# GpSimd's product of q held behind VectorE's keys, and a second scan tile, in a gated linear attention with a feed-forward layer

## The chip, the cores and the metric

One core of one Trainium2 chip runs the whole kernel. The metric is the device time of one execution in microseconds (us). TensorE is called PE, VectorE DVE, ScalarE ACT, GpSimd POOL, and SyncE, which issues most DMAs, SP, as in the profile.

## The reference

```python
for t in range(S):
    state = alpha[:, :, t, :, None] * state + np.einsum('bhd,bhe->bhde', k[:, :, t], v[:, :, t])
    y[:, :, t] = np.einsum('bhd,bhde->bhe', q[:, :, t], state)
...
h = x @ w_in
g = 0.5 * h * (1.0 + erf(h * inv_sqrt2))
return (g @ w_out).astype(np.float32)
```

There are 4 batches, 8 heads, 768 steps and head dimension 48; alpha lies between 0.8 and 1. The attention's output, as 3072 tokens by 384, goes through a feed-forward layer with 2048 hidden units, all in float32.

## The kernel before

**Attention in units.** Tokens are cut into 12 groups of 256, three to a batch. A group has two units of four heads each; unit n is u = n % 2 of group g = n // 2, so there are 24. In names of `pp`, `rp`, `pe`, `s` and `ss`, such as `pp_7_1`, the first figure is the group and the second is u (here unit 15); in those of `hp`, `ghi` and `glo` they are group and hidden slice. A last figure only tells buffers apart. For each unit:

- DVE makes running products of alpha forward (`pp`, two scans, L283), takes the last of them (L287, L289), makes running products backward (`rp`, two scans, L304), and multiplies k by `rp` in place. This last product is called the keys (L309).
- q is multiplied by `pp` into a tile `qk` (L299): on DVE in units 0 to 5, on POOL from unit 6 on, the late units. There are three `qk` tiles in turn, so the product of unit n needs the tile that unit n - 3 has read for the last time.
- PE makes scores from `qk` and the keys (L325), DVE masks them (`ss`, L340), PE multiplies them by v (L399) and makes the sums for the states (L426), DVE adds the states up (L452, L454), and PE multiplies q by the states (L487, the outer part). ACT and DVE turn the result into the high and low parts of x (L541, L545).

**Late units on PE come in visits.** The visit of unit n runs, in this order, L399 of unit n, L426 of unit n + 1, L325 of unit n + 2, a short POOL memset called `done` that waits for PE (L842), and L487 of unit n, which waits for that memset.

**Feed-forward in steps.** A step `3_4` is hidden slice 4 of group 3. gemm1 (L572, 18 matmuls) fills `hp`; ACT takes the gelu twice, to `ghi` (L593) and in place (L594); DVE makes `glo`, their difference (L599); gemm2 (L622, 12 matmuls) multiplies `ghi` by the weights' high and low parts and then, in its last four matmuls, `glo`.

**The order is written out by a planner.** `plan_unit` makes an `Op` for every piece of work with an engine, a cost, dependencies and a rank. A loop places them on PE, DVE, ACT, SP and POOL by costs from a table (`COST`, for example 1.35 for POOL's product, 0.65 for keys), and the instructions are issued in the order planned. So one dependency more moves work on other engines too. On the chip only semaphores hold an instruction: within an engine the order is fixed, across engines each waits for the data that it uses and for the buffers that it writes. `pp` and `rp` have one buffer each. In the plan the first forward scan of a unit waits for the product of the unit before, since that product reads `pp`:

```python
pp = work.tile([P, 2, G], F32, tag="pp", bufs=1, name=f"pp_{g}_{u}")
...
d["first"] = op("DVE", "scan", start, [d["load"], p.get("q"), p.get("back")], rank=r)
...
before = pp_.get("outer") if n < NU * NSB + 2 else unit[n - 3].get("outer")
d["q"] = op(e, cost, lambda: fns["q"](), [d["scan"], d["rest"], before], rank=r)
```

Here `p` is the unit before, `pp_` the one before that, and `before` the outer part of unit n - 3. The keys are not among the product's dependencies.

Of the kernel before, what the change touches and what calls it, by code (L numbers as in the profile page):

```python
# [8 lines left out]
F32 = mybir.dt.float32  # L9
# [6 lines left out]
ALU = mybir.AluOpType  # L16
AX = mybir.AxisListType
PSUM = bass.MemoryType.PSUM
# [12 lines left out]
LANES = 8  # L31
RATE, ALONE, LATENCY, SMALL, BEGIN = 350e3, 290e3, 2.1, 50e3, 2.2
MARGIN = 1.5
HOME = {0: 0, 1: 1, 2: 2, 4: 1, 5: 0, 6: 2, 8: 1, 9: 0, 10: 2, "s": 1}
X_GAP, Z_GAP, HI_GAP, LO_GAP, LATE_GAP = (128, 0, 192), 0, (64, 0), (0, 64), 0
COST = dict(
    scan=0.65, back=0.72, keys=0.65, q=1.35, qv=0.62, scores=1.0, kn=0.5, mask=0.62, inside=1.05, chain=1.15, outer=0.85, carry=0.26, last=0.34, last_p=0.15, sums=0.55, scaled=0.45,
# [7 lines left out]
def gla_then_gelu_ffn(ctx: ExitStack, tc: tile.TileContext, q, k, v, alpha, akq, w_in, w_out, out):  # L45
    nc = tc.nc
    B, H, D, S = q.shape
    NF, P, NK, _ = w_in.shape
# [3 lines left out]
    G = 2 * C  # L52
    CS = C // 2
# [3 lines left out]
    NU = NPAIR // 2  # L57
# [4 lines left out]
    NSB = GPB  # L62
# [78 lines left out]
    for half in range(2):  # L141
        r = slice(half * CS, (half + 1) * CS)
        nc.gpsimd.affine_select(
            out=mask[r],
# [16 lines left out]
    late = []  # L161
# [107 lines left out]

    cur = {}  # L270

    def ahead(g, u):
        at, kt, qt = (data[g % NB][:, u, n] for n in range(3))
        pp = work.tile([P, 2, G], F32, tag="pp", bufs=1, name=f"pp_{g}_{u}")
        rp = work.tile([P, 2, G], F32, tag="rp", bufs=1, name=f"rp_{g}_{u}")
        pe = work.tile([P, 2], F32, tag="pe", bufs=6, name=f"pe_{g}_{u}")
        cur[g, u] = dict(pe=pe, kt=kt)

        def by_chunk(x):
            return x.rearrange("p i (j t) -> p i j t", t=CS)  # L280

        def forward(i):
            nc.vector.tensor_tensor_scan(pp[:, i], at[:, i], top, MID, ALU.mult, ALU.min)  # L283

        def last():
            eng = nc.vector if g >= NSB else nc.gpsimd
            eng.tensor_scalar(out=pe, in0=pp[:, :, G - 1], scalar1=BOTTOM, scalar2=None, op0=ALU.max)  # L287
            if g >= NSB:
                nc.vector.reciprocal(rp[:, :, G - 1], pe)  # L289

        def queries():
            n = NU * g + u
            if len(qk) == NU and n >= NU * NSB + 2:
                to_late()
                qk.append(late[0].tile([P, 2, NCH, KW], F32, tag="qk2", name="qk2"))
                put_eye(qk[-1])
            qs = cur[g, u]["qs"] = qk[u if g < NSB else n % (NU + 1)]
            eng = nc.vector if g < NSB else nc.gpsimd
            eng.tensor_tensor(out=qs[:, :, :, :CS], in0=by_chunk(qt), in1=by_chunk(pp), op=ALU.mult)  # L299

        def backward(i):
            if g < NSB and i == 0:
                nc.vector.reciprocal(rp[:, :, G - 1], pe)
            nc.vector.tensor_tensor_scan(  # L304
                rp[:, i, G - 2 :: -1], at[:, i, G - 1 : 0 : -1], top[:, 1:], rp[:, i, G - 1 :], ALU.mult, ALU.min
            )

        def keys():
            nc.vector.tensor_tensor(out=kt, in0=kt, in1=rp, op=ALU.mult)  # L309

        return forward, queries, backward, last, keys

# [456 lines left out]
    def op(*args, **kw):  # L769
        ops.append(Op(*args, **kw))  # L770
        return ops[-1]
# [4 lines left out]
    def plan_unit(n):  # L776
# [21 lines left out]
        else:  # L798
            d["v"] = p["v"]
        pool = g < NSB  # L800
        d["first"] = op("DVE", "scan", start, [d["load"], p.get("q"), p.get("back")], rank=r)
        d["scan"] = op("DVE", "scan", lambda: fns["f"](1), [d["first"]], rank=r)
        d["last"] = op("POOL" if pool else "DVE", "last_p" if pool else "last", lambda: fns["l"](), [d["scan"]], rank=r)
        e, cost = ("DVE", "qv") if pool else ("POOL", "q")
# [7 lines left out]
        d["back"] = op("DVE", "keys", lambda: fns["k"](), [d["b1"], d["rest"]], rank=r)  # L812
        if pool:
            d["b0"].cost += 0.17
        ready = [d["back"], d["q"], p.get("mask"), p.get("kn")]
        if pool or n == NU * NSB:
            d["scores"] = op("PE", "scores", lambda: scores(g, u), ready, rank=r)
# [345 lines left out]
```

## Time and profile before

| what | value |
|---|---|
| median of 3 runs | 503.26 us (502.67 to 503.4) |
| the profiled execution | 503.02 us |
| its span | 501.0 us |
| PE busy | 487.1 us, 97% |
| DVE busy | 301.7 us, 60% |
| POOL busy | 34.8 us, 7% |
| mean granted PE clock | 0.995 of full speed |

Times in the trace count from the start of the span. A row of a timeline gives start, duration, engine, line, operation, what is written and read, and how many instructions; in brackets stands the engine's idle time before, and what ended it. Matmuls overlap, so the duration of a row is not the step from one matmul to the next.

### The profile page before, as it was taken

What the parts mean: (1) busy time and instruction counts of PE and PEld (TensorE: products, weight loads), DVE (VectorE), ACT (ScalarE), POOL (GpSimd) and SP (SyncE); (2) the same over time, 40 slices, a digit from 0 to 9 for tenths busy, and PEclk for the clock granted to TensorE, in tenths of its full rate; (3) what the DMA queues carried; (4) which work ended last, traced back from release to release, by engine and by line L of the source; (5) the groups of instructions that cost most, each with busy time, mean ns of one, the idle gap of its engine ahead of it and who ended that gap; (6) DMA issues with size and microseconds to landing.
All of it is one profiled execution on the core that took longest, in us unless ns stands there. A gap on an engine that the chain in (4) does not pass through costs nothing.

```text
span 501.0 us, 13833 instructions
## 1 busy us (share of the span) xinstructions
PE 487.1 (97%) x5970; PEld 474.9 (95%) x5970; DVE 301.7 (60%) x580; ACT 217.9 (43%) x467; POOL 34.8 (7%) x69
## 2 busy tenths in 40 slices
PE   7898999999999999999999999999999999999996
PEld 7777899999998999998999999999999999999996
DVE  6999999999789999899266264251232211211211
ACT  2776856645445555555352352351332222222221
POOL 4100011000111121211010011000000000000000
PEclk9998999999999999999999999999999999999999
DMA  8967363531024453344031020010010000000001
GB/s 299 391 189 236 123 234 128 188 128 65 0 89 147 139 170 120 103 163 143 1 86 60 2 82 2 0 49 2 1 46 4 0 33 1 33 0 1 33 0 37
DMA packets 17153, 44.20 MB, mean 88 GB/s; under 512 B 2240, under 2 KB 8512, under 8 KB 17088
## 3 DMA queue, kind: packets, MB, share of 16 engines
q1 hardware_dynamic: 16656, 42.87, 25.3%
q8 instruction: 49, 0.80, 0.7%
q10 hardware_dynamic: 432, 0.39, 0.3%
q14 instruction: 16, 0.13, 0.1%
HBM read 36.18 MB, written 4.72 MB: 82 GB/s over the span
## 4 chain that ended last, share of the span: by engine, by line
PE 85%; DVE 9%; issue 2%; ACT 1%; DMA 1%; SPq 0%; DVEq 0%
PE acc L622 38%; PE hp L572 38%; PE s L325 3%; PE ybank L399 2%; PE ybank L487 2%; DVE rp L304 2%; DVE pp L283 2%; PE ybank L426 2%; DMA akq<-in_akq_dram 1%; DVE qk L299 1%; DVE ss L340 1%; DVE x L545 1%; DVE glo L599 1%; DVE akq L309 0%; DVE states L454 0%
## 5 line engine op out<-in xcount | busy, mean ns | idle before, releaser
L572 PE MATMUL hp<-x,wih 128*128 128x256 f32 x1152 | 202.5, 278 | 0.0
L572 PEld LDWEIGHTS hp<-x,wih 128*128 128x128 f32 x1152 | 179.2, 189 | 0.6
L572 PE MATMUL hp<-x,wil 128*128 128x256 f32 x576 | 159.8, 278 | 0.0
L599 DVE TENSOR_TENSOR glo<-hp,ghi 128x512 fp32r<-128x512 f32 x92 | 63.1, 686 | 160.4 <-ACT hp L594 160.3
L593 ACT ACTIVATE ghi<-hp 128x512 fp32r<-128x512 f32 x96 | 57.4, 598 | 197.7 <-PE hp L572 197.4
L622 PE MATMUL acc<-woh,ghi 128*128 128x384 f32 x384 | 130.9, 341 | 0.0
L622 PE MATMUL acc<-wol,ghi 128*128 128x384 f32 x384 | 128.9, 336 | 0.0
L572 PEld LDWEIGHTS hp<-x,wil 128*128 128x128 f32 x576 | 108.9, 189 | 0.0
L622 PE MATMUL acc<-woh,glo 128*128 128x384 f32 x384 | 82.5, 335 | 2.0 <-DVE glo L599 2.0
L622 PEld LDWEIGHTS acc<-woh,ghi 128*128 128x128 f32 x384 | 72.1, 188 | 1.7
L622 PEld LDWEIGHTS acc<-wol,ghi 128*128 128x128 f32 x384 | 72.1, 188 | 0.0
L622 PEld LDWEIGHTS acc<-woh,glo 128*128 128x128 f32 x384 | 67.8, 188 | 2.8 <-DVE glo L599 2.7
L594 ACT ACTIVATE hp<-hp 128x512 f32<-128x512 f32 x96 | 56.9, 593 | 0.0
L304 DVE TENSOR_TENSOR_SCAN rp<-akq,rp,top 128x255 f32<-128x255 f32 x48 | 35.8, 774 | 0.8
L283 DVE TENSOR_TENSOR_SCAN pp<-akq,top 128x256 f32<-128x256 f32 x48 | 31.0, 679 | 3.9 <-POOL qk L299 2.0
L299 POOL TENSOR_TENSOR qk<-akq,pp 128x512 f32<-128x512 f32 x18 | 24.8, 1380 | 45.8 <-DVE pp L283 15.5
L325 PE MATMUL s<-qk,akq 48*64 48x112 f32 x768 | 23.9, 260 | 2.3 <-DVE akq L309 1.1
L541 ACT CAST x<-ybank 64x256 fp32r<-64x256 f32 (+4 forms) x60 | 20.0, 333 | 9.4 <-PE ybank L487 5.0
L334 ACT COPY kn<-s 128x384 f32<-128x384 f32 x24 | 11.5, 480 | 28.9 <-DVE ss L340 16.3
L454 DVE TENSOR_TENSOR states<-ybank,states 128x96 f32<-128x96 f32 x66 | 16.8, 255 | 10.1 <-ACT x L541 7.8
L309 DVE TENSOR_TENSOR akq<-akq,rp 128x512 f32<-128x512 f32 x24 | 22.2, 926 | 0.7
L325 PEld LDWEIGHTS s<-qk,akq 48*64 48x64 f32 x768 | 19.3, 133 | 3.2 <-issue 1.5
(79 smaller groups left out, 390.3 us busy)
## 6 DMA issues: line engine op xcount, KB each, us to landing
akq<-in_akq_dram SPq DMA_DIRECT2D x22, 768.0 KB, 5.2
st<-in_moe_w_in_dram SPq DMA_DIRECT2D x8, 768.0 KB, 4.4
st<-in_moe_w_out_dram SPq DMA_DIRECT2D x8, 768.0 KB, 4.9
vn<-in_v_dram SPq DMA_DIRECT2D x12, 384.0 KB, 4.9
out_dram<-part SPq DMA_DIRECT2D x11, 384.0 KB, 3.0
x<-z SPq DMA_DIRECT2D x63, 32.0 KB, 1.9
akq<-in_akq_dram SPq DMA_DIRECT2D x2, 512.0 KB, 5.2
akq<-in_akq_dram SPq DMA_DIRECT2D x2, 256.0 KB, 4.5
```

Of the source, the lines that this page charges most:

```text
L283: nc.vector.tensor_tensor_scan(pp[:, i], at[:, i], top, MID, ALU.mult, ALU.min)
L299: eng.tensor_tensor(out=qs[:, :, :, :CS], in0=by_chunk(qt), in1=by_chunk(pp), op=ALU.mult)
L304: nc.vector.tensor_tensor_scan(rp[:, i, G - 2 :: -1], at[:, i, G - 1 : 0 : -1], top[:, 1:], rp[:, i, G - 1 :], ALU.mult, ALU.min)
L309: nc.vector.tensor_tensor(out=kt, in0=kt, in1=rp, op=ALU.mult)
L325: nc.tensor.matmul(d["s"][o, h, e : e + KW], lhsT=d["kt"][r, i, t], rhs=d["qs"][r, i, j], start=True, stop=True)
L454: d["chain"] = nc.vector.tensor_tensor(out=st[j + 1], in0=new, in1=st[j], op=ALU.add)
L541: nc.scalar.copy(hi, y)
L572: nc.tensor.matmul(hp[:, j, :], lhsT=a[:, j, i * P : (i + 1) * P], rhs=x[:, i, :], start=(j == 0 and i == 0 and n == 0), stop=(i == NK - 1 ...
L593: nc.scalar.activation(ghi, hp, AF.Gelu)
L594: nc.scalar.activation(hp, hp, AF.Gelu)
L599: nc.vector.tensor_tensor(out=glo, in0=hp, in1=ghi.bitcast(F32), op=ALU.subtract)
L622: nc.tensor.matmul(acc[t], lhsT=a[:, j, t * C : (t + 1) * C], rhs=w[:, j, :], start=(first and j == 0 and k == 0 and w is wo_hi[f]), stop= ...
```

## The change

Three things change, all for late units. The instruction of POOL's product gets a dependency on the keys of its own unit, and so does its `Op` in the plan. The odd units from 11 on take their `pp` from a pool on the side that the weights' conversion has left (`late`), so that `pp` of an odd and of an even unit are two tiles. In the plan the first forward scan then waits for the product of two units before, where either this unit or the one before has the second tile, which is so from unit 11 on.

```diff
--- before.py
+++ after.py
@@ -31,6 +31,7 @@
 LANES = 8
 RATE, ALONE, LATENCY, SMALL, BEGIN = 350e3, 290e3, 2.1, 50e3, 2.2
 MARGIN = 1.5
+OTHER_FROM = 11
 HOME = {0: 0, 1: 1, 2: 2, 4: 1, 5: 0, 6: 2, 8: 1, 9: 0, 10: 2, "s": 1}
 X_GAP, Z_GAP, HI_GAP, LO_GAP, LATE_GAP = (128, 0, 192), 0, (64, 0), (0, 64), 0
 COST = dict(
@@ -269,9 +270,13 @@
 
     cur = {}
 
+    def other_products(n):
+        return n >= OTHER_FROM and n % 2 == 1
+
     def ahead(g, u):
         at, kt, qt = (data[g % NB][:, u, n] for n in range(3))
-        pp = work.tile([P, 2, G], F32, tag="pp", bufs=1, name=f"pp_{g}_{u}")
+        room = late[0] if other_products(NU * g + u) else work
+        pp = room.tile([P, 2, G], F32, tag="pp", bufs=1, name=f"pp_{g}_{u}")
         rp = work.tile([P, 2, G], F32, tag="rp", bufs=1, name=f"rp_{g}_{u}")
         pe = work.tile([P, 2], F32, tag="pe", bufs=6, name=f"pe_{g}_{u}")
         cur[g, u] = dict(pe=pe, kt=kt)
@@ -296,7 +301,14 @@
                 put_eye(qk[-1])
             qs = cur[g, u]["qs"] = qk[u if g < NSB else n % (NU + 1)]
             eng = nc.vector if g < NSB else nc.gpsimd
-            eng.tensor_tensor(out=qs[:, :, :, :CS], in0=by_chunk(qt), in1=by_chunk(pp), op=ALU.mult)
+            ins = eng.tensor_tensor(out=qs[:, :, :, :CS], in0=by_chunk(qt), in1=by_chunk(pp), op=ALU.mult)
+            if g >= NSB:
+                tc.add_manual_dep(
+                    ins.ins,
+                    cur[g, u]["keys"].ins.name,
+                    mybir.DependencyInfo(mybir.DependencyClass.Sync, mybir.DependencyReason.DATA),
+                    reason="beside instructions that read PSUM",
+                )
 
         def backward(i):
             if g < NSB and i == 0:
@@ -306,7 +318,7 @@
             )
 
         def keys():
-            nc.vector.tensor_tensor(out=kt, in0=kt, in1=rp, op=ALU.mult)
+            cur[g, u]["keys"] = nc.vector.tensor_tensor(out=kt, in0=kt, in1=rp, op=ALU.mult)
 
         return forward, queries, backward, last, keys
 
@@ -798,7 +810,7 @@
         else:
             d["v"] = p["v"]
         pool = g < NSB
-        d["first"] = op("DVE", "scan", start, [d["load"], p.get("q"), p.get("back")], rank=r)
+        d["first"] = op("DVE", "scan", start, [d["load"], (p if not other_products(n) and not other_products(n - 1) else pp_).get("q"), p.get("back")], rank=r)
         d["scan"] = op("DVE", "scan", lambda: fns["f"](1), [d["first"]], rank=r)
         d["last"] = op("POOL" if pool else "DVE", "last_p" if pool else "last", lambda: fns["l"](), [d["scan"]], rank=r)
         e, cost = ("DVE", "qv") if pool else ("POOL", "q")
@@ -812,6 +824,8 @@
         d["back"] = op("DVE", "keys", lambda: fns["k"](), [d["b1"], d["rest"]], rank=r)
         if pool:
             d["b0"].cost += 0.17
+        else:
+            d["q"].deps.append(d["back"])
         ready = [d["back"], d["q"], p.get("mask"), p.get("kn")]
         if pool or n == NU * NSB:
             d["scores"] = op("PE", "scores", lambda: scores(g, u), ready, rank=r)
```

The sequence of instructions on POOL stays as it was. On DVE, ACT, PE and SP the planner gives other places to some. Line numbers of the changed program are higher: the forward scan is L288, `pe` L292, its reciprocal L294, POOL's product L304, the backward scan L316, keys L321, scores L337, L399 is L411, L426 is L438, states L464 and L466, the outer part L499, gemm1 L584, `glo` L611 and gemm2 L634.

The listing shows the scans as SCALAR_TENSOR_TENSOR. First, DVE between the visits of units 10 and 13, from the forward scans of unit 15 on. Before:

```order
L283 SCALAR_TENSOR_TENSOR pp_7_1_2804<-akq1_119,top_113 128x256 x2
L287 TENSOR_SCALAR pe_7_1_2806<-pp_7_1_2804 128x2
L289 RECIPROCAL rp_7_1_2805<-pe_7_1_2806 128x2
L304 SCALAR_TENSOR_TENSOR rp_7_1_2805<-akq1_119,rp_7_1_2805,top_113 128x255 x2
L309 TENSOR_TENSOR akq1_119<-akq1_119,rp_7_1_2805 128x512
L599 TENSOR_TENSOR glo_3_5_2899<-hp_3_5_2808,ghi_3_5_2894 128x512
L452 COPY states1_132<-ybank_137 128x96
L454 TENSOR_TENSOR states1_132<-ybank_137,states1_132 128x96 x3
```

With the change, from the keys of unit 14 on:

```order
L321 TENSOR_TENSOR akq1_119<-akq1_119,rp_7_0_2616 128x512
L288 SCALAR_TENSOR_TENSOR pp_7_1_2689<-akq1_119,top_113 128x256 x2
L292 TENSOR_SCALAR pe_7_1_2691<-pp_7_1_2689 128x2
L294 RECIPROCAL rp_7_1_2690<-pe_7_1_2691 128x2
L316 SCALAR_TENSOR_TENSOR rp_7_1_2690<-akq1_119,rp_7_1_2690,top_113 128x255
L611 TENSOR_TENSOR glo_3_4_2766<-hp_3_4_2668,ghi_3_4_2760 128x512
L316 SCALAR_TENSOR_TENSOR rp_7_1_2690<-akq1_119,rp_7_1_2690,top_113 128x255
L464 COPY states0_131<-ybank_137 128x96
```

Before, the forward scans of unit 15 stood behind the reads of a visit, and their backward scans, keys and then `glo` of step 3_5 followed each other. Now they stand directly behind the keys of unit 14, `glo` of step 3_4 stands between the two backward scans, and the keys of unit 15 come later.

Second, PE at the visit of unit 10, from the matmul ahead of it on. Before:

```order
L572 MATMUL hp_3_2_2496<-x3_1973,wil2_148 128x256
L399 MATMUL ybank_137<-ss_5_0_2303,vn1_118 64x64 x16
L426 MATMUL ybank_137<-vn1_118,kn_127 64x48 x12
L325 MATMUL s_6_0_2551<-qk0_120,akq0_117 64x112 x16
L487 MATMUL ybank_137<-qk1_121,states0_131 48x64 x16
L572 MATMUL hp_3_3_2593<-x3_1973,wih3_141 128x256 x2
```

With the change:

```order
L584 MATMUL hp_3_3_2523<-x3_1973,wil3_149 128x256
L411 MATMUL ybank_137<-ss_5_0_2302,vn1_118 64x64 x16
L438 MATMUL ybank_137<-vn1_118,kn_127 64x48 x12
L337 MATMUL s_6_0_2578<-qk0_120,akq0_117 64x112 x16
L499 MATMUL ybank_137<-qk1_121,states0_131 48x64 x16
L634 MATMUL acc0_3_0_2437<-woh2_156,ghi_3_2_2542 128x384
```

Before, the visit stood behind gemm1 of step 3_2 and ahead of gemm1 of step 3_3; now it stands behind both, and gemm2 of step 3_2 follows it at once.

Third, PE at the visit of unit 11. Before:

```order
L399 MATMUL ybank_137<-ss_5_1_2463,vn1_118 64x64 x16
L426 MATMUL ybank_137<-vn0_116,kn_127 64x48 x16
L325 MATMUL s_6_1_2707<-qk1_121,akq0_117 64x112 x16
L487 MATMUL ybank_137<-qk2_1849,states1_132 48x64 x16
L622 MATMUL acc0_3_0_2437<-woh3_157,ghi_3_3_2640 128x384
```

With the change:

```order
L411 MATMUL ybank_137<-ss_5_1_2462,vn1_118 64x64 x16
L438 MATMUL ybank_137<-vn0_116,kn_127 64x48 x16
L337 MATMUL s_6_1_2726<-qk1_121,akq0_117 64x112 x16
L499 MATMUL ybank_137<-qk2_1849,states1_132 48x64 x16
L634 MATMUL acc0_3_0_2437<-woh4_158,ghi_3_4_2760 128x384
```

The visit was followed by gemm2 of step 3_3 and is now followed by gemm2 of step 3_4, since the visits of units 10 and 11 stand one step later among the steps.

## Rows read from the trace of the kernel before

**Rows 1.** The page's head: span, and busy time of PE, the weight load and VectorE.
```profile
span 501.0 us, 13833 instructions
...
PE 487.1 (97%) x5970; PEld 474.9 (95%) x5970; DVE 301.7 (60%) x580; ACT 217.9 (43%) x467; POOL 34.8 (7%) x69
```

**Rows 2.** Busy time in stretches of 20 us; columns as in the first row.
```profile
core 0: us, PE busy (x) PEld busy (x) DVE busy (x) ACT busy (x) POOL busy (x), PEclk, DMA share, GB/s
...
220.00:240.00 20.00, 18.96 (x262) 18.36 (x252) 17.55 (x36) 8.85 (x22) 2.79 (x3) 1.00 0.34 109
...
380.00:400.00 20.00, 20.00 (x147) 20.00 (x146) 3.94 (x7) 5.44 (x10) 0.00 (x0) 1.00 0.00 1
```

**Rows 3.** Waits of PE: who for whom, us in total, times, longest.
```profile
PE acc L622 <- DVE glo L599: 2.0, 2, 1.0
```

**Rows 4.** POOL's product of q by its line: duration in ns, min/median/max.
```profile
L299 POOL TENSOR_TENSOR qk<-akq,pp x18: 1290/1306/1737, 63.2 to 300.5; 128x512 f32<-128x512 f32 x18
```

**Rows 5.** VectorE's backward scans by their line: duration in ns, min/median/max.
```profile
L304 DVE TENSOR_TENSOR_SCAN rp<-akq,rp,top x48: 721/745/1832, 6.5 to 300.1; 128x255 f32<-128x255 f32 x48
```

**Rows 6.** VectorE's keys by their line, columns as above.
```profile
L309 DVE TENSOR_TENSOR akq<-akq,rp x24: 684/692/1691, 7.9 to 300.9; 128x512 f32<-128x512 f32 x24
```

**Rows 7.** Timeline of VectorE from 149 to 232 us.
```profile
start us, us, engine line op out<-in xcount [idle before <-releaser]
149.61 0.67 DVE L599 TENSOR_TENSOR glo<-hp,ghi 128x512 fp32r<-128x512 f32 x1
150.19 1.23 DVE L309 TENSOR_TENSOR akq<-akq,rp 128x512 f32<-128x512 f32 x1
...
158.34 1.83 DVE L304 TENSOR_TENSOR_SCAN rp<-akq,rp,top 128x255 f32<-128x255 f32 x1
160.09 0.66 DVE L599 TENSOR_TENSOR glo<-hp,ghi 128x512 fp32r<-128x512 f32 x1
...
164.73 0.69 DVE L309 TENSOR_TENSOR akq<-akq,rp 128x512 f32<-128x512 f32 x1
165.33 1.27 DVE L283 TENSOR_TENSOR_SCAN pp<-akq,top 128x256 f32<-128x256 f32 x2
...
229.56 1.61 DVE L309 TENSOR_TENSOR akq<-akq,rp 128x512 f32<-128x512 f32 x1
231.09 0.68 DVE L599 TENSOR_TENSOR glo<-hp,ghi 128x512 fp32r<-128x512 f32 x1
```

**Rows 8.** Timeline of PE at two waits and at one visit (start, us).
```profile
160.81 0.44 PE L622 MATMUL acc<-woh,glo 128*128 128x384 f32 x1 [0.99 <-DVE glo L599]
...
165.78 0.69 PE L399 MATMUL ybank<-ss,vn 64*64 64x64 f32 x32
...
166.75 0.95 PE L325 MATMUL s<-qk,akq 48*64 48x112 f32 x30
...
168.07 0.44 PE L622 MATMUL acc<-woh,ghi 128*128 128x384 f32 x1
...
231.82 0.97 PE L622 MATMUL acc<-woh,glo 128*128 128x384 f32 x4 [1.04 <-DVE glo L599]
```

**Rows 9.** Timeline of POOL in the same stretch; in brackets its idle time before.
```profile
149.57 1.30 POOL L299 TENSOR_TENSOR qk<-akq,pp 128x512 f32<-128x512 f32 x1 [1.06 <-PE ybank L487]
...
158.32 1.30 POOL L299 TENSOR_TENSOR qk<-akq,pp 128x512 f32<-128x512 f32 x1 [1.09 <-PE ybank L487]
...
185.72 1.74 POOL L299 TENSOR_TENSOR qk<-akq,pp 128x512 f32<-128x512 f32 x1 [1.09 <-PE ybank L487]
...
211.86 1.72 POOL L299 TENSOR_TENSOR qk<-akq,pp 128x512 f32<-128x512 f32 x1 [1.09 <-DMA x<-z]
...
229.30 1.32 POOL L299 TENSOR_TENSOR qk<-akq,pp 128x512 f32<-128x512 f32 x1 [1.12 <-PE ybank L487]
```

**Rows 10.** Waits of POOL: us in total, times, longest.
```profile
POOL qk L299 <- PE ybank L487: 12.3, 11, 1.4
```

## Prediction

> **What bounds the kernel now.** I read the head of the page first: PE is busy for 487.1 of 501.0 us [rows 1]. So a change on POOL and DVE can give only what PE waits for them, or take what it makes PE wait. Second, the busy time by stretches: from 220 to 240 us DVE is busy for 17.55 of 20 us and PE has lost 1.04, while from 380 to 400 DVE has 3.94 us of work and PE loses nothing [rows 2]. The change can act only while late units are made, and there DVE has little to spare. Third, the waits of PE: for `glo` it waited twice, 2.0 us in all [rows 3]. Fourth, the timelines, for what made `glo` late. One backward scan took 1.83 us where the median is 745 ns; it started at 158.34, beside a product that ran from 158.32 to 159.62, and the `glo` behind it started at 160.09 [rows 5, 7, 9]. PE sat idle for 0.99 us and went on at 160.81 [rows 8]. The second wait is alike: keys took 1.61 us from 229.56, beside a product from 229.30 to 230.62, `glo` began at 231.09, and PE waited 1.04 us [rows 7 to 9]. So an instruction of DVE with both inputs in SBUF (a scan, the keys) is held while POOL's product runs. The price of a meeting is 1832 - 745 = 1.09 us for a scan [rows 5] and up to 1691 - 692 = 1.00 us for keys [rows 6]. `glo`, which reads one input from PSUM, took 0.67 us at 149.61 beside the product of 149.57 [rows 7, 9]: it isn't held. When DVE is first, POOL waits: products of 1.74 and 1.72 us against a median of 1.306, 0.42 more [rows 4, 9].
>
> **What is removed.** The product no longer runs beside backward scans and keys of its own unit, so the two meetings that made PE wait are gone: -2.0 us [rows 3]. That is all there is to gain. Other keys were held too (1.23 us at 150.19 [rows 7]), but PE didn't wait for `glo` after them.
>
> **What is added: the product is later.** It starts when its unit's keys end, and PE's scores wait for it. At unit 11 the keys ended at 164.73 + 0.69 = 165.42 and the bulk of the visit's scores started at 166.75 [rows 7, 8], 1.33 us later. A product of 1.306 us [rows 4] just fits; one that first lets a scan by takes 1.74 [rows 9], 0.41 too long. DVE and PE both come there about 1 us earlier with the change, so their distance stays. The next forward scan starts at 165.33, before the keys end [rows 7], so DVE is first: I take 0.4, between 0 and 0.4. Behind the waiting product on POOL stands the visit's `done`, and behind that PE's outer part; scores wait in the same visit already, so this adds nothing. In the unit after it the second forward scan meets the rest of the product and loses about the 1.0 us that its backward scan no longer loses: no change, between -1 and +1 in DVE's time, with gemm work as cover.
>
> **What is moved.** From unit 11 on two tiles of `pp` let DVE run one unit ahead: forward scans stand directly behind the keys of the unit before (the first of the places shown). The keys of a unit are then done before the visit that gives back its `qk` tile, and the product waits for that visit as it does today, when PE's outer part ended its wait 11 times, some 1.1 us before its start [rows 9, 10]. It then runs beside the scans or keys of the **next** unit, which nothing in the change keeps apart from it. So meetings are as many as before, about one to a visit; what counts is whether the held instruction stands ahead of the `glo` that gemm2 directly behind the visit needs. In both waits of today it did. I find three such places in the new order, where the product of unit n is let go by the visit of unit n - 3. After the visit of unit 11 the product of unit 14 meets the first backward scan of unit 15, and `glo` of step 3_4 is next, for the gemm2 shown behind that visit. After the visit of unit 13 the product of unit 16 meets a backward scan of unit 17; the unit's keys stand between it and the `glo` that is needed. After the visit of unit 15 the product of unit 18 meets the keys of unit 19, with `glo` directly behind. The first and third I price as the two measured waits, 1.0 us each [rows 8]. The second costs 1.0 and the keys' 0.60 us (164.73 to 165.33 [rows 7]): 1.6. Sum 3.6. Each can also be nothing, as when the scan starts first and POOL waits, or as much as a hold and keys, 1.7 us; so 0 to 5.1.
>
> On the size of a hold the row and the notes differ a little. The Trainium skill, SBUF — State Buffer, section Who interferes with whom, says that the second to issue fully blocks until the first has finished; a scan that starts with the product would then take 1.306 + 0.745 = 2.05 us, and by that three waits would be 0.7 us dearer in all. The row of 158.34 shows 1.83, and I go by it.
>
> Without effect: the second tile itself; the moves of visits and conversions between 64 and 130 us, where PE waits for nothing and the same work stays on each engine; swapped loads and stores on SP, since the operands that they bring are used many steps later. Work on PE is the same, with as many visits, and after the last visit gemm work alone is left to the end, as in the stretch from 380 us [rows 2].
>
> **Sum.** -2.0 + 0.4 + 3.6 = +2.0 us. On the profiled execution's 503.02 us that is 505.0. The median of the runs is 0.24 higher, 503.26, so the forecast for it is **505.3 us**. A measurement of this kernel tells about 0.2%, 1.0 us, from no change.
>
> **Rivals.**
> - *It does what its words say, and PE's waits go.* If keys really come last, the product runs beside `glo`, states and masks, and DVE gets its holds back. For it: `glo` isn't held, and the two waits are both of this kind. Against it: the new order puts forward scans, not reads of PSUM, behind the keys of units 11, 12, 14, 15 and 18. The decisive point is whether the keys of units 14 to 18 end after the outer part that frees the tile. Result: 503.26 - 2.0 = 501.3 us; with one of the three waits, 502.3. The Trainium skill, same page and section, says that an instruction with at most one SBUF input doesn't contend with GpSimd; by that alone this rival would come true, and the trace agrees with it for `glo`.
> - *As many waits as before.* Two of the three places make PE wait 1.0 us, the scores nothing: -2.0 + 2.0, 503.3 us, between 502.3 and 504.2. For it: not all held keys cost PE a wait today, and 0.1 us decides whether DVE or POOL comes first. Against it: the second place has two instructions ahead of `glo`.
> - *Everything waits.* Three dear places and the scores: -2.0 + 0.4 + 5.1 = +3.5, 506.8 us. For it: DVE has some 10% to spare in these visits, so it doesn't make up a hold by the next visit.
>
> **How the numbers follow.** I give 0.62 to slower by over 1.0 us (my forecast, about 504.3 to 506.4 by itself, and the last rival, 0.10 of it), 0.24 to as many waits, 0.14 to the first rival. The range reaches from 502.0, which leaves out most of the first rival, to 507.0, just over the last.
>
> **What would show it.** Right: in the trace after, PE's waits for `glo` number three or so and sum to over 3 us, each behind a scan or keys of over 1 us beside a product; POOL's product is still let go by PE's outer part in units 14 to 18; scores of unit 11 wait for POOL. Wrong: products start with the end of keys everywhere, scans and keys stay near 745 and 692 ns, and PE's waits for `glo` are gone. If holds stay and PE doesn't wait, my choice of places is wrong; if PE waits elsewhere, for the masks or for x, a move that I costed at nothing is.

## The result, and the profile after

The change made the kernel slower: 508.02 us median of 6 runs (506.6 to 509.2) against 503.06 us (502.43 to 503.62) for the kernel before in the same measurement, a ratio of 1.0096 with a 95% interval of 1.0075 to 1.0117. That is 5.0 us; 2.0 were forecast, and the range ended at 507.0. The profiled execution took 506.6 us, so it is the quickest of the six, and a part of what the median lost need not be in it. The two executions of the change with a mean granted PE clock of 0.999, the profiled one among them, took 506.6 and 506.7 us, and the four with 0.993 to 0.997 took 507.8 to 509.2.

The head of the page, against [rows 1]:

```profile
span 504.7 us, 13831 instructions
PE 487.6 (97%) x5970; PEld 474.4 (94%) x5970; DVE 301.5 (60%) x580; ACT 217.2 (43%) x467; POOL 35.7 (7%) x69
```

PE's work is about the same (487.1 before), so what was lost are PE's waits. From 60 to 260 us they are (line waited for, us in total, times, longest), against [rows 3]:

```profile
PE acc L634 <- DVE glo L611: 3.8, 2, 2.4
PE hp L584 <- DMA x<-z: 1.4, 1, 1.4
PE ybank L411 <- DVE x L557: 0.4, 1, 0.4
PE s L337 <- POOL done L856: 0.2, 1, 0.2
```

The two waits for `glo` that PE had before [rows 8] are gone, and two others have come. Where time goes can be read from the start of each gemm1 step in both traces. The step at 153.70 us before starts at 154.70 after, the one at 242.94 at 246.69, and from there to the end of PE's work nothing more is lost. So 2.75 us go between 154 and 247 us, and up to 1.0 us in the early stretch. Of this 1.0 us, 0.38 is there at the first gemm1 step (31.93 before), ahead of any late unit. Then the change comes to lie 1.16 us ahead, at the step of 50.59 us before, because of PE's clock: the gemm1 step ahead of it took from 45.72 to 50.59 us before, 4.87 us, and 3.50 us in the change. From 40 to 60 us the mean granted clock was 0.91 in the kernel before and 1.00 in the change (third figure from the end of each row; before, then after):

```profile
40.00:60.00 20.00, 17.80 (x240) 16.26 (x242) 18.84 (x32) 14.59 (x30) 0.21 (x1) 0.91 0.56 184
40.00:60.00 20.00, 17.61 (x294) 15.92 (x292) 19.59 (x33) 15.45 (x32) 0.21 (x1) 1.00 0.57 190
```

So the kernel before ran a part of this stretch at the lower of the two levels, 1.2 instead of 2.4 GHz. From 40 to 45 us PE had been busy for 3.50 us in either kernel, at the full clock, so these traces show no reason for the fall. The change loses its lead again, most of it by the wait for x; it is 0.62 us behind at the step of 78.75 us before, and 1.00 at that of 121.61.

The first new wait, in the timelines of DVE, POOL and PE (rows as in [rows 7 to 9]):

```profile
187.26 1.27 DVE L288 TENSOR_TENSOR_SCAN pp<-akq,top 128x256 f32<-128x256 f32 x2
188.56 1.14 DVE L292 TENSOR_SCALAR pe<-pp 128x2 f32<-128x2 f32 x1
189.74 0.17 DVE L294 RECIPROCAL rp<-pe 128x2 f32<-128x2 f32 x1
189.94 0.75 DVE L316 TENSOR_TENSOR_SCAN rp<-akq,rp,top 128x255 f32<-128x255 f32 x1
190.60 0.67 DVE L611 TENSOR_TENSOR glo<-hp,ghi 128x512 fp32r<-128x512 f32 x1
```
```profile
188.38 1.29 POOL L304 TENSOR_TENSOR qk<-akq,pp 128x512 f32<-128x512 f32 x1 [1.09 <-PE ybank L499]
```
```profile
191.33 0.96 PE L634 MATMUL acc<-woh,glo 128*128 128x384 f32 x4 [1.45 <-DVE glo L611]
```

The product of unit 14 is let go by PE's outer part, not by its keys, which ended 1.04 us before it started, and runs beside the next unit's work. The held instruction is the tiny `pe` of 128x2: 1.14 us, where its row in the view of one line has a median of 169 ns. Everything up to `glo` shifts by 1 us.

The second new wait has two parts:

```profile
221.59 0.68 DVE L321 TENSOR_TENSOR akq<-akq,rp 128x512 f32<-128x512 f32 x1
223.48 1.27 DVE L288 TENSOR_TENSOR_SCAN pp<-akq,top 128x256 f32<-128x256 f32 x2 [1.20 <-DMA akq<-in_akq_dram]
225.19 2.38 DVE L316 TENSOR_TENSOR_SCAN rp<-akq,rp,top 128x255 f32<-128x255 f32 x2
227.61 0.69 DVE L321 TENSOR_TENSOR akq<-akq,rp 128x512 f32<-128x512 f32 x1
228.22 0.68 DVE L611 TENSOR_TENSOR glo<-hp,ghi 128x512 fp32r<-128x512 f32 x1
```
```profile
225.09 1.30 POOL L304 TENSOR_TENSOR qk<-akq,pp 128x512 f32<-128x512 f32 x1 [1.12 <-PE ybank L499]
```
```profile
228.96 0.97 PE L634 MATMUL acc<-woh,glo 128*128 128x384 f32 x4 [2.38 <-DVE glo L611]
```

Two backward scans beside the product of unit 18 take 2.38 us, where two undisturbed ones take 1.39:

```profile
205.93 1.39 DVE L316 TENSOR_TENSOR_SCAN rp<-akq,rp,top 128x255 f32<-128x255 f32 x2
```

And DVE had come so far ahead that its forward scan, that of unit 19, waited 1.20 us for the unit's data. SP shows why these came late. Before:

```profile
207.07 3.67 SPq L564 DMA_DIRECT2D x<-z  x6
210.83 0.54 SPq L653 DMA_DIRECT2D out_dram<-part  x1
211.53 3.88 SPq L164 DMA_DIRECT2D akq<-in_akq_dram  x2
```

With the change, and under it what SP waited for at L665 (in us, times, longest):

```profile
213.83 0.40 SPq L665 DMA_DIRECT2D out_dram<-part  x1
214.32 4.42 SPq L576 DMA_DIRECT2D x<-z  x6
218.91 1.02 SPq L165 DMA_DIRECT2D akq<-in_akq_dram  x2
```
```profile
SPq L665 <- DVE part L653: 7.4, 1, 7.4
```

The load was issued 7.4 us later than before, while the scan that needs it started 2.95 us earlier (223.48 instead of 226.43). DVE ended `z`, which the six transfers carry, 4.5 us later than before (at 211.84 instead of 207.31), since the visits stand later among the steps. Most of the other 2.9 us comes from the store of `part`: it has moved ahead of the six, SP waited for `part` until 213.83 us, and the six and the load waited behind it.

In all, products were held up more often than before: from 150 to 240 us five took over 1.5 us, where two did before. The first row is theirs (line, operation, count, min/median/max ns, start of the first and last; against [rows 4]); by the second, PE's outer part still ended most of their waits, as in [rows 10]:

```profile
L304 POOL TENSOR_TENSOR qk<-akq,pp x18: 1282/1300/1769, 70.3 to 304.2; 128x512 f32<-128x512 f32 x18
```
```profile
POOL qk L304 <- PE ybank L499: 12.0, 11, 1.1
```

### The profile page after: what moved, and what is told of

Its sections match the earlier page's. It is cut to its first block, busy times and chain, and to the rows that moved or that the text cites. A ratio compares the mean times of both kernels' runs of the same rounds, so it can differ in the third digit from the quotient of the medians.

```text
span 504.7 us, 13831 instructions
## 1 busy us (share of the span) xinstructions
PE 487.6 (97%) x5970; PEld 474.4 (94%) x5970; DVE 301.5 (60%) x580; ACT 217.2 (43%) x467; POOL 35.7 (7%) x69
## 4 chain that ended last, share of the span: by engine, by line
PE 79%; DVE 11%; DMA 3%; issue 3%; ACT 2%; ACTq 1%; POOL 0%; SPq 0%; DVEq 0%; POOLq 0%
PE hp L584 35%; PE acc L634 35%; PE s L337 3%; DVE pp L288 2%; PE ybank L411 2%; PE ybank L499 2%; DMA akq<-in_akq_dram 2%; DVE rp L316 1%; DMA x<-z 1%; PE ybank L438 1%; DVE states L466 1%; DVE glo L611 1%; DVE ss L352 1%; DVE x L557 1%; PE ybank L379 1%
## 5 line engine op out<-in xcount | busy, mean ns | idle before, releaser
L584 PE MATMUL hp<-x,wih 128*128 128x256 f32 x1152 | 201.0, 277 | 1.4 <-DMA x<-z 1.4
L584 PEld LDWEIGHTS hp<-x,wih 128*128 128x128 f32 x1152 | 178.0, 188 | 2.0 <-issue 1.6
L611 DVE TENSOR_TENSOR glo<-hp,ghi 128x512 fp32r<-128x512 f32 x92 | 63.1, 685 | 162.8 <-ACT hp L606 162.8
L584 PE MATMUL hp<-x,wil 128*128 128x256 f32 x576 | 159.2, 276 | 0.0
L634 PE MATMUL acc<-woh,ghi 128*128 128x384 f32 x384 | 131.3, 342 | 0.0
L634 PE MATMUL acc<-wol,ghi 128*128 128x384 f32 x384 | 128.9, 336 | 0.0
L584 PEld LDWEIGHTS hp<-x,wil 128*128 128x128 f32 x576 | 108.2, 188 | 0.0
L634 PE MATMUL acc<-woh,glo 128*128 128x384 f32 x384 | 82.5, 335 | 3.8 <-DVE glo L611 3.8
L634 PEld LDWEIGHTS acc<-woh,ghi 128*128 128x128 f32 x384 | 72.0, 188 | 2.1
L634 PEld LDWEIGHTS acc<-wol,ghi 128*128 128x128 f32 x384 | 72.1, 188 | 0.0
L634 PEld LDWEIGHTS acc<-woh,glo 128*128 128x128 f32 x384 | 67.8, 188 | 4.6 <-DVE glo L611 4.5
L288 DVE TENSOR_TENSOR_SCAN pp<-akq,top 128x256 f32<-128x256 f32 x48 | 33.0, 721 | 5.8 <-DMA akq<-in_akq_dram 3.8
L316 DVE TENSOR_TENSOR_SCAN rp<-akq,rp,top 128x255 f32<-128x255 f32 x48 | 35.5, 768 | 0.8
L304 POOL TENSOR_TENSOR qk<-akq,pp 128x512 f32<-128x512 f32 x18 | 25.2, 1397 | 64.6 <-PE acc L634 22.4
L337 PE MATMUL s<-qk,akq 48*64 48x112 f32 x768 | 24.3, 260 | 1.8 <-PE ybank L499 0.7
L466 DVE TENSOR_TENSOR states<-ybank,states 128x96 f32<-128x96 f32 x66 | 16.8, 255 | 10.5 <-ACT x L553 7.7
L337 PEld LDWEIGHTS s<-qk,akq 48*64 48x64 f32 x768 | 19.5, 133 | 3.1 <-issue 1.2
L557 DVE TENSOR_TENSOR x<-ybank,x 64x256 fp32r<-64x256 f32 (+3 forms) x54 | 19.2, 355 | 2.4 <-ACT x L553 1.5
```

The costliest lines, as they stand in the source:

```text
L304: ins = eng.tensor_tensor(out=qs[:, :, :, :CS], in0=by_chunk(qt), in1=by_chunk(pp), op=ALU.mult)
L316: nc.vector.tensor_tensor_scan(rp[:, i, G - 2 :: -1], at[:, i, G - 1 : 0 : -1], top[:, 1:], rp[:, i, G - 1 :], ALU.mult, ALU.min)
L337: nc.tensor.matmul(d["s"][o, h, e : e + KW], lhsT=d["kt"][r, i, t], rhs=d["qs"][r, i, j], start=True, stop=True)
L466: d["chain"] = nc.vector.tensor_tensor(out=st[j + 1], in0=new, in1=st[j], op=ALU.add)
L557: nc.vector.tensor_tensor(out=lo, in0=y, in1=hi.bitcast(F32), op=ALU.subtract)
L584: nc.tensor.matmul(hp[:, j, :], lhsT=a[:, j, i * P : (i + 1) * P], rhs=x[:, i, :], start=(j == 0 and i == 0 and n == 0), stop=(i == NK - 1 ...
```

## The experiments

The theory after the result: the second tile, with its looser dependency in the plan, lets the planner put DVE's scans a unit ahead. A unit's keys are then done before its `qk` tile is free, the dependency on the keys holds nothing back, and the product runs beside scans and keys of the next unit, ahead of a `glo` that PE needs. Rivals: the wait for the keys itself costs; the new order costs, with or without meetings; the early move costs. Ratios are to the kernel before, measured beside it (503.02 to 503.43 us).

| kernel | us, median | ratio, 95% interval |
|---|---|---|
| the change | 508.02 | 1.0096 (1.0075 to 1.0117) |
| e1: units 6 and 7 as before | 506.77 | 1.0073 (1.0053 to 1.0093) |
| e2: order of the change, no wait | 506.17 | 1.0063 (1.0042 to 1.0085) |
| e3: the change, memset for product | 501.81 | 0.9965 (0.9953 to 0.9977) |
| e4: before, memset for product | 500.18 | 0.9938 (0.9922 to 0.9955) |
| e5: keys, one tile | 502.50 | 0.9991 (0.9981 to 1.0001) |
| e6: second tile alone | 505.87 | 1.0054 (1.0038 to 1.0070) |
| e7: before, product after states | 500.63 | 0.9952 (0.9935 to 0.9969) |
| e8: before, product in halves | 500.40 | 0.9953 (0.9936 to 0.9969) |
| e9: keys, two tiles, old plan | 502.85 | 0.9992 (0.9979 to 1.0005) |
| e10: keys from unit 8, one tile | 501.41 | 0.9962 (0.9949 to 0.9976) |
| e11: the change, product in halves | 506.35 | 1.0059 (1.0041 to 1.0077) |
| e12: second tile, product after states | 500.56 | 0.9944 (0.9922 to 0.9967) |

**e1, the early units as before.**

```diff
-            if g >= NSB:
+            if NU * g + u >= 8:
                 tc.add_manual_dep(
...
-        else:
+        elif n >= 8:
             d["q"].deps.append(d["back"])
```

> The dependency on the keys, in the plan and on the instruction, is kept from unit 8 on and taken away for units 6 and 7; the second tile stays. PE's order up to 100 us is then that of the kernel before, the rest nearly that of the change. Theory (the early move costs by itself): gemm1 at 72 us no longer stands directly behind the step before it, its wait of 1.4 us for x is gone, and with the two short waits of the scores of units 6 and 7 (0.6 us) the time falls by 1.4 to 2.0 us against the change, to 506.0 to 506.6 us. Rival (only meetings of POOL and DVE cost, all after 160 us): the wait for x is made up elsewhere and the time stays at 508 us.

The time fell by about 1.2 us, but the intervals overlap, and the expected reason didn't hold: at the step of gemm1 that waited for x PE waits again. The view names no releaser here.

```profile
PE hp L584 <- issue: 1.3, 1, 1.3
```

So PE's order around that step matters little. The next step of gemm1 starts at 78.76 us here, at 79.37 in the change. In the kernel before, with the same order there, it started at 78.75 without this wait; that execution had come to this stretch later, by the lower clock. The profiled execution of e1 shows one thing more. With the order of the change behind 110 us, `glo` is late a third time:

```profile
207.02 1.60 DVE L321 TENSOR_TENSOR akq<-akq,rp 128x512 f32<-128x512 f32 x1
208.54 0.68 DVE L611 TENSOR_TENSOR glo<-hp,ghi 128x512 fp32r<-128x512 f32 x1
```
```profile
206.53 1.53 POOL L304 TENSOR_TENSOR qk<-akq,pp 128x512 f32<-128x512 f32 x1 [1.06 <-PE ybank L499]
```
```profile
209.27 0.97 PE L634 MATMUL acc<-woh,glo 128*128 128x384 f32 x4 [1.22 <-DVE glo L611]
```

In the profile of the change the same keys started 0.3 us ahead of the same product, took 0.69 us, and PE waited for nothing there. A few tenths of a microsecond decide whether a meeting costs 1.2 us or nothing.

**e2, the order alone.**

```diff
-            if g >= NSB:
+            if False:
                 tc.add_manual_dep(
...
```

> Everything of the change stays, its order on every engine and the second tile, but POOL's instruction no longer waits for the keys. Theory (the new order costs, not the wait): from unit 14 on PE's outer part lets the product go after the keys anyway, so the waits for glo at 190 and 228 us and the wait for x at 72 us stay; only the scores of unit 11 no longer wait (0.2 us). 507.5 us, between 507.0 and 508.3. Rival (the wait on the instruction is what costs): back to 503 to 504.5 us, without waits for glo over 1 us.

Measured 506.17 us, 0.8 below the theory's range and far above the rival's. PE waits for `glo` three times, 4.4 us in all. The wait on the instruction costs at most 1.9 us (508.02 - 506.17); the order without it costs 2.7 (506.17 - 503.43).

**e3 and e4, no meetings.** Both leave out the product of q in the late units.

```diff
-            ins = eng.tensor_tensor(out=qs[:, :, :, :CS], in0=by_chunk(qt), in1=by_chunk(pp), op=ALU.mult)
+            ins = eng.memset(qs[:, :, :, :CS], 0.5) if g >= NSB else eng.tensor_tensor(out=qs[:, :, :, :CS], in0=by_chunk(qt), in1=by_chunk(pp), op=ALU.mult)
```

The cut shows e3; the edit of e4 is the same in the kernel before.

> The change, with POOL's product of q in late units replaced by a POOL memset of the same tile, which reads nothing; it leaves out the product of q with the running products of alpha in units 6 to 23. All orders and waits stay. Theory (held instructions of DVE make glo late): no scan, keys or pe is over 1 us beside the memset, PE's waits for glo (3.8 us) and x of DVE (0.4 us) go, and the early wait for x by DMA (1.4 us) stays: 508.0 - 4.2 = 503.8 us, between 503.2 and 504.6. Rival (the new order has glo too late whether or not anything is held): at least 2 us of waits for glo remain, 506 us or more.

> The kernel before with the same replacement: POOL's product of q in late units becomes a memset of the same tile; it leaves out the product of q with the running products of alpha in units 6 to 23. Theory (PE's two waits for glo in the kernel before come from held instructions): they go and the time falls by 2.0 us to 501.1 us, between 500.7 and 501.5. With e3 this tells what the change costs without any meeting: 503.8 - 501.1 = 2.7 us by the theory. Rival (what is won from holds comes back as a wait elsewhere): 502.5 us or more.

Both came out quicker than expected, 501.81 and 500.18 us. A memset is also shorter, about 0.53 us against 1.30, but from 150 to 245 us DVE waits for no product in either kernel, so the length alone gives little there (at most PE's wait of 0.2 us for `done`). The meetings are worth 2.9 to 3.3 us in the kernel before (503.06 or 503.43 - 500.18) and 6.2 us in the change (508.02 - 501.81), and without them the change is 1.6 us dearer. PE's only wait for `glo` left in e3 is as long: a forward scan, again that of unit 19, waits for its load, and `glo` stands behind it; DVE first, then PE:

```profile
219.36 1.27 DVE L288 TENSOR_TENSOR_SCAN pp<-akq,top 128x256 f32<-128x256 f32 x2 [2.19 <-DMA akq<-in_akq_dram]
```
```profile
PE acc L634 <- DVE glo L611: 1.6, 1, 1.6
```

The early wait for x, which the theory kept, wasn't there in e3; whether the memset took it away or it differs between executions isn't shown.

**e5, keys with one tile.**

```diff
-OTHER_FROM = 11
+OTHER_FROM = 99
```

> The change without the second tile: one buffer for the forward scans in all units, the dependency of POOL's product on the keys stays from unit 6 on. Theory (the second tile lets DVE run ahead; forward scans of units ahead then wait for akq's DMA in front of glo and meet the product of the unit before): with one tile a forward scan cannot start before the product ends, so DVE waits no more for akq's DMA (2.1 us in the change) and products start at the end of the keys, beside glo, masks and x. PE's waits for glo fall from 3.8 us to under 1.2; what stays of the early move is 0.6 to 1.0 us: 503.0 to 504.5 us. Rival (waiting for the keys is what costs, with either number of tiles): 506 us or more, with scores of PE that wait for POOL.

Measured 502.50 us, below the range. The dependency now does what its words say. The keys end 11 waits of POOL, and no scan or keys is held in the whole program (min/median/max ns):

```profile
POOL qk L304 <- DVE akq L321: 47.3, 11, 8.3
```
```profile
L316 DVE TENSOR_TENSOR_SCAN rp<-akq,rp,top x48: 722/742/750, 6.2 to 298.6; 128x255 f32<-128x255 f32 x48
```
```profile
L321 DVE TENSOR_TENSOR akq<-akq,rp x24: 681/691/693, 7.6 to 299.4; 128x512 f32<-128x512 f32 x24
```

Against [rows 5, 6] the maxima fall from 1832 and 1691 to 750 and 693. PE waits for `glo` nowhere from 60 to 260 us; it waits once for x from DMA (1.0) and once for x from DVE (0.9). DVE waits for the product instead, 7.1 us in five places from 150 to 245 us, and that is mostly covered.

**e6, the second tile alone.**

```diff
-            if g >= NSB:
+            if False:
                 tc.add_manual_dep(
...
-        else:
-            d["q"].deps.append(d["back"])
```

> The second tile and its looser dependency in the plan alone; POOL's product waits for no keys, in the plan or on the chip. PE's order is that of the kernel before up to 240 us, but for one swap. Theory (the tile is what costs): at least two waits of PE for glo of over 1 us between 185 and 230 us, one of them behind a scan that waits for akq's DMA; 505.0 to 506.3 us, as much as the kernel with the change's order and no wait on the chip. Rival (the wait for the keys costs, the tile gives room): 502 to 503.5 us.

Measured 505.87 us, in the theory's range. From 150 to 245 us PE waits for `glo` four times and for x once:

```profile
PE acc L634 <- DVE glo L611: 3.8, 4, 1.4
PE ybank L411 <- DVE x L557: 0.8, 1, 0.8
```

So the tile with its plan costs 2.8 us (505.87 - 503.07) without any wait for keys, and 5.5 us with it (508.02 - 502.50).

**e7, after the states.** The product waits for DVE's last addition to the states instead; behind it on DVE stand the masks and the reads of x.

```diff
...
+            if NU * g + u >= 9:
+                tc.add_manual_dep(
+                    ins.ins,
+                    cur[g - 1, u]["chain"].ins.name,
...
+        if n >= 9:
+            d["q"].deps.append(pp_["chain"])
```

> A version of the kernel before, with one tile: from unit 9 on the product of q of unit n waits, in the plan and on the chip, for DVE's last addition to the states of unit n - 2 in the visit that frees its qk tile, since the masks and the reads of x stand behind that addition and read PSUM. Theory (a meeting costs only beside instructions with both inputs in SBUF): products lie beside masks and x reads, no scan and no keys are over 1.2 us from 150 to 240 us, PE's two waits for glo (2.0 us) go, and the time comes near that of the kernel without any meeting, 500.2 us: 500.2 to 501.5. Rival (a later product makes the one tile the bound: the next forward scan waits for it and glo behind that scan is late): 503 us or more.

Measured 500.63 us, 2.4 below the kernel before and 7.4 below the change. One of these products, on POOL and beside it on DVE:

```profile
160.65 1.30 POOL L299 TENSOR_TENSOR qk<-akq,pp 128x512 f32<-128x512 f32 x1 [3.48 <-DVE states L461]
```
```profile
160.43 0.68 DVE L347 TENSOR_TENSOR ss<-s,mask 128x512 f32<-128x512 f32 x1
161.03 1.28 DVE L552 TENSOR_TENSOR x<-ybank,x 128x256 fp32r<-128x256 f32 x3
```

The product fits beside the masks and x, nobody is held, and from 60 to 260 us PE has no wait that the view lists.

**e8, halves.**

```diff
...
+            else:
+                for i in range(2):
+                    eng.tensor_tensor(out=qs[:, i, :, :CS], in0=by_chunk(qt)[:, i], in1=by_chunk(pp)[:, i], op=ALU.mult)
```

> The kernel before with POOL's product in two instructions of 128x256 each. Theory (a held instruction waits for the rest of one POOL instruction, and DVE gets the port between two): a held scan or keys is at most 0.7 us longer instead of 1.1, PE's two waits for glo fall from 1.0 to some 0.5 us each: 502.2 us, between 501.5 and 503.0. Rival (both halves hold, one after the other, or hold one instruction more): as before, 503.2 to 504.2 us.

Measured 500.40 us, below the range. The longest backward scan takes 1268 ns instead of 1832, and PE's two waits for `glo` shrink from 2.0 us to 0.6:

```profile
L308 DVE TENSOR_TENSOR_SCAN rp<-akq,rp,top x48: 716/744/1268, 6.0 to 297.3; 128x255 f32<-128x255 f32 x48
```
```profile
PE acc L626 <- DVE glo L603: 0.6, 2, 0.3
```

That explains 1.4 of the 2.4 us by the ratio. In the two traces the rest is one step of gemm1, which took from 45.72 to 50.59 us in the kernel before and from 45.54 to 49.01 in e8; the mean granted clock from 45 to 50 us was 0.66 there and 1.00 here. So it needn't come from the halves.

**e9, two tiles with the old plan.**

```diff
-        d["first"] = op("DVE", "scan", start, [d["load"], (p if not other_products(n) and not other_products(n - 1) else pp_).get("q"), p.get("back")], rank=r)
+        d["first"] = op("DVE", "scan", start, [d["load"], p.get("q"), p.get("back")], rank=r)
```

> The change with one line put back: in the plan the first forward scan of a unit waits for the product of the unit before again, in all units. The second tile stays in memory and the product waits for the keys, so the order on every engine is that of the kernel with one tile (502.5 us). Theory (it is the looser dependency in the plan that puts scans a unit ahead, not the tile in memory): 502.5 us, between 501.8 and 503.4, no wait of PE for glo over 1 us, no wait of DVE for akq's DMA; a forward scan behind the keys meets the product instead of waiting for it, which costs about the same. Rival (the second tile itself, its place in memory or the scans that it lets start on the chip, costs): 505 us or more.

Measured 502.85 us, as e5, and PE's waits for `glo` sum to 0.2 us. The tile in memory is harmless; the looser dependency in the plan is what costs.

**e10, keys from unit 8, one tile.** The edits of e1 and e5 together.

> One tile, and the dependency on the keys from unit 8 on alone, so that units 6 and 7 and PE's order up to 100 us are those of the kernel before. Theory (the early move costs by itself, as it did with two tiles, where units 6 and 7 taken out gave back about 1.2 us): 501.5 us, between 501.0 and 502.0. Rival (early moves are covered by the later landing of x, which ends at the same time either way): 502.5 us as with one tile and the dependency from unit 6.

Measured 501.41 us, as the theory had it, and the interval lies apart from that of e5. So the early units cost 1.1 us. The traces point to the wait on the instruction, and not to the moves alone: between the gemm1 steps that start at 78.75 and 121.61 us before, the kernels in which the products of units 6 and 7 wait for their keys lose 0.38 us (the change), 0.34 (e5), 1.27 (e9) and 1.35 (e11). All others lose at most 0.11; e2, with the moves but without that wait, loses 0.05. The products, started later, meet other instructions of the weights' conversion than before: `u` (L213), a tensor_scalar, is held twice in the change, where it takes 1.12 and 1.21 us, and not in e10, where `w` (L219) is held once instead, as before. Here is `u` in the change and in e10:

```profile
L213 DVE TENSOR_SCALAR u<-u x16: 532/552/1205, 13.2 to 129.0; 128x768 int32<-128x768 int32 x16
```
```profile
L213 DVE TENSOR_SCALAR u<-u x16: 533/552/560, 12.9 to 127.3; 128x768 int32<-128x768 int32 x16
```

How much of such holds reaches PE isn't shown.

**e11, the change in halves.** The edit of e8 in the changed kernel, each half with its dependency on the keys.

> The change with POOL's product in two instructions of 128x256, each with the dependency on the keys; the order on the other engines is that of the change. Theory (what is dear in the change is mostly the hold: 6.2 us between it and the kernel with memsets): an instruction of DVE is held for at most 0.5 us instead of 1.1, PE's waits for glo fall from 3.8 to 2.5 us or less, of which the scan's wait for akq's DMA keeps some 1.3; 503.0 to 505.0 us. Rival (scans a unit ahead are too early for their data and too far ahead of glo, holds or not): 506.5 us or more.

Measured 506.35 us, outside the theory's range and just under the rival's. Halves save 1.7 of 6.2 us only. The reason is in DVE's timeline at the second place: the first half holds `pe`, the second the scan behind it, and the wait for the load stays.

```profile
225.22 1.27 DVE L288 TENSOR_TENSOR_SCAN pp<-akq,top 128x256 f32<-128x256 f32 x2 [1.29 <-DMA akq<-in_akq_dram]
226.52 0.74 DVE L292 TENSOR_SCALAR pe<-pp 128x2 f32<-128x2 f32 x1
227.30 0.17 DVE L294 RECIPROCAL rp<-pe 128x2 f32<-128x2 f32 x1
227.51 1.62 DVE L319 TENSOR_TENSOR_SCAN rp<-akq,rp,top 128x255 f32<-128x255 f32 x2
```

**e12, second tile, product after the states.** The tile and the plan of e6, the dependency of e7. Its order on every engine is that of e6; only the moment of the product differs.

> The second tile with its looser dependency in the plan, and in place of the dependency on the keys that on the last addition to the states, as in the version after the states, from unit 9 on. The order on every engine is that of the kernel with the tile alone (505.9 us); only the moment of POOL's product on the chip differs. Theory (with scans a unit ahead most of the cost is meetings, and the rest forward scans that wait for akq's DMA in front of glo): no instruction of DVE is held for over 0.3 us between 150 and 240 us, the wait for akq's DMA of 1 to 2 us stays and one wait of PE for glo behind it: 501.0 to 502.5 us, that is at least 3.4 us less than the tile alone and up to 1.9 us more than the version after the states with one tile (500.6 us). Rival (the looser plan costs by its order, meetings or not): 503.5 us or more.

Measured 500.56 us, 5.3 below e6, under the theory's range. PE waits for `glo` nowhere from 60 to 260 us, although a forward scan waits longer for its load than in the change:

```profile
DVE pp L288 <- DMA akq<-in_akq_dram: 2.6, 1, 2.6
```

So in this order, with scans a unit ahead, the whole cost is meetings. The wait of 2.6 us stands at unit 21 (233.65 us), where the change waits 0.90 us for its load and PE for nothing. The load of unit 19 isn't late here: the order on SP is that of the kernel before. In the order of the change that load costs PE time without any meeting too (1.6 us in e3).

## Why the prediction fell short

The direction was right, and so was the mechanism of the late stretch. The size was not.

- *The two waits removed, -2.0.* Right: both are gone in the change, in e5 and in e10.
- *Scores of unit 11, +0.4.* Right: PE's wait in that visit is 0.2 us, and the step of gemm1 behind it loses 0.42 us against that of before.
- *Three places, +3.6.* The profile shows 1.45, nothing and 2.38, in all 3.8. The sum is near, but not by its parts. At the first, `pe` was held in place of the scan behind it. At the second, DVE came first, the lower end that the text gave; e1 shows it at 1.22, so the change can pay it in other executions. At the third the hold cost its 1.0, and a wait for akq's load that wasn't forecast 1.2 on top. It was costed nowhere, though the text said that scans go a unit ahead: the load and its place on SP's queue had to be asked for as well.
- *Reads of x.* A late x of DVE held up the visit at 185 us by 0.4 us. This cost wasn't in the sum.
- *"Without effect: ... the moves of visits and conversions between 64 and 130 us; swapped loads and stores on SP".* **This is the step that failed: two terms put at nothing.** For the early units the argument was that PE waits for nothing there before. They cost 1.1 us by e10 against e5, clear of noise, and 1.2 by e1 against the change, not clear of it. PE's wait of 1.4 us for x isn't the proof that it looks like, since e1 has one of 1.3 with the order of before. For SP the argument was that the operands are used many steps later. With scans ahead that isn't so: visits that stand later, and a store swapped ahead of the transfers of x, made the load of unit 19 late, which took 1.2 us of DVE's time in the change and 1.6 us of PE's in e3.
- *The rest.* -2.0 + 0.4 + 3.8 + 0.4 is 2.6, near the 2.75 us that the profile loses after 154 us; with 1.1 for the early units the sum is 3.7, and the profiled execution was 3.6 us longer than that of before. This closeness is in part luck, since 0.38 us of the difference stands ahead of any late unit. The medians differ by 5.0, and what makes up the other 1.3 us stays open. Executions of the change with three waits are one candidate, since e1, with the same order, shows the second place at 1.2; no profile of the change has it. The other is PE's clock, by which the executions of the change differ.
- *"The second tile itself" at nothing.* e9 bears this out for the tile in memory; the plan around it costs 5.5 us where the product waits for the keys.
- *The first rival* (the words come true) is what one tile gives: e10 is at 501.4 us, where 501.3 was worked out. The deciding point that the text named, whether the keys end after the outer part, was the right one.

The prediction also drew on the page "SBUF — State Buffer" of the Trainium skill, section Who interferes with whom, for the rule that an instruction with at most one SBUF input doesn't contend. It left out the rule's exception, DVE's two-port modes, which the page says tensor_scalar can enter. `glo`, masks and the reads of x agree with the rule; `pe`, a tensor_scalar with one input, was held for 0.97 us, `u` for 0.65, and both agree with the exception. That an instruction with two inputs doesn't contend with one on POOL that only writes, from the same section, agrees with the memsets of e3 and e4: keys take 695 ns at most there, backward scans 824.

## What to carry to other kernels

A dependency that keeps two instructions apart works only as long as it is the last to be met. Ask what else in the change lets one of them run ahead, and which other wait then decides the moment: here a second buffer made the keys early, and PE's outer part brought the product beside the next unit's scans. Tie the guarded instruction to the one that stands directly ahead of its safe cover (the states, ahead of masks and x): that beat both kernels, with one tile or two.

## What was not expected of the hardware

- A 128x2 tensor_scalar on DVE with one input in SBUF took 1.14 us beside POOL's product, against 0.17 alone. A hold doesn't shrink with the held instruction. Its row names no wait, so it isn't only semaphores that hold an instruction here, as the section on the kernel before has it: an instruction of another engine does too.
- Between two scans that DVE has ready POOL doesn't always get in: the longest product took 1769 ns, 0.47 over the median. It started in the first of two scans and ended 1.08 us behind the second.

```profile
174.20 1.27 DVE L288 TENSOR_TENSOR_SCAN pp<-akq,top 128x256 f32<-128x256 f32 x2
```
```profile
174.78 1.77 POOL L304 TENSOR_TENSOR qk<-akq,pp 128x512 f32<-128x512 f32 x1 [7.85 <-PE hp L584]
```

- Two products of 128x256 (0.75 us each at the median) instead of one of 1.30 hold a scan for 0.52 us (1268 - 744) instead of 1.09, with nothing else changed; but each half can hold an instruction of its own.
